# A decode layer on one core: 128 rows of w4 loaded to 16 partitions by eight two-partition loads, the rest in groups of 5, 4, 3 and 1

## The chip, the cores and the metric

The kernel runs on one core of a Trainium2 chip. The metric is device time in microseconds of one execution; the figure of a kernel is the median of several runs.

## What is computed

The reference is one decode step (sequence length 1, batch 8, D = 512): attention over the last 2048 positions of a K/V cache, then an MLP block. Cut to what matters:

```python
x = A_x                                       # [8, 1, 512]
h = x + attention(layernorm(x), k[..., -2048:, :], v[..., -2048:, :], wq, wo)
x1 = h_n + 0                                  # h_n = layernorm(h); the token-shift branch is zero for S = 1
h2 = gelu(layernorm(x1) @ w3) @ w4            # w3 [512, 1792], w4 [1792, 512]
out = h + x1 + h2
```

There are 32 query heads in 8 groups, and each group has its own K and V (head size 128). All of K, V, wq, wo, w3 and w4 that is used comes from HBM once: some 79 MB, of which w3 and w4 are 1.75 MB each. Everything is bf16, with sums in f32.

## The kernel before

One Python function writes out the instruction list of every engine by hand; `Engine.op` (L46) appends an operation with the semaphores it waits for, and `Engine.emit` (L52) writes them in that order. The engines are TensorE (`PE`), ScalarE (`AC`), VectorE (`DV`), GpSimd (`PO`) and SyncE (`SP`). SP issues every large load, in one queue, in program order.

**Ring.** `ring` (L122) has 8 slots of 2 MB. 32 loads of 2 MB, half a batch's K or V each, go round it in the order of `loads` (L292). A load into a slot waits until TensorE has used what was there (`taken`). wq and wo share another buffer. w3 and w4 go into ring slots 0 and 1 at the end: `w3_sb`, `w4_sb` (L124, L125). The order in SP's queue at the end is: the last K and V loads, four of wo, two of w3 (L669), four of w4 (L675).

**Attention.** For each of 64 steps, K is transposed on TensorE (`pe_T`, L317), evicted by ScalarE and VectorE (`evict`, L333) and multiplied by the queries (`pe_QK`, L339). The softmax is spread over the steps; GpSimd multiplies P by a mask (L384). `pe_PV` (L438) multiplies by V. `wo` follows in `pe_wo` (L543). `stream` (L593) adds filler matmuls of 512 columns at places where TensorE would wait.

**The tail.** After wo, VectorE makes the layernorm's sums (L685 to L700) and `uT`, the transposed input of w3. `pe_w3` (L705) holds 128 columns of w3 as weights and moves `uT`; w3 comes in two halves of its 512 rows, each with a semaphore, and there is one call for the first half (L715) and two for the second (L717). Its columns are taken in *chunks* of 128: as w4's load puts `r` consecutive rows of w4 on each partition, chunk `i` of a group has every `r`-th column of w3:

```python
w4_chunks += [slice(f0 + i, f0 + 128 * r, r) for i in range(r)]
dma(SP, w4_sb[:, lo:lo + r, :].rearrange("p r n -> p (r n)"),
    B_w4[f0:f0 + 128 * r, :].rearrange("(p r) n -> p (r n)", r=r), sem, w_free[1] if lo == 0 else None)
```

The groups before are r = 8, 3, 2 and 1, 14 chunks in all. The first 8 go to one PSUM bank with 64 moving columns, the other 6 to another with 32. VectorE multiplies each bank by the row scale (L738), ScalarE applies gelu (L741), and `pe_w4` (L751) holds 128 x 8 of the result as weights and moves w4, two matmuls per chunk, one for each half of the 512 outputs, on two column halves of the array. Residual and normalised input are added by `pe_fin` (L761), two filler matmuls follow (L768), then w4 group by group as it lands (L769). VectorE and ScalarE evict a half each (L774), SP stores (L778).

## Time and profile before

| | us |
|---|---|
| median of 3 runs | 193.57 (193.43 to 193.58) |
| the profiled execution | 193.76 |
| its span in the profile | 192.3 |
| TensorE busy | 159.8 (83%) |
| VectorE busy | 103.8 (54%) |
| ScalarE busy | 84.4 (44%) |
| GpSimd busy | 35.8 (19%) |
| large loads' packets, of 16 DMA engines' span | 97.0% |
| chain that ended last, DMA's share | 78% |

The profile is one execution, and its times count from the first instruction. In its rows, PE is TensorE's matmul, PEld its weight load, DVE VectorE, ACT ScalarE, POOL GpSimd, SPq the queue of SyncE; `L325` is a line of the kernel. A row of the timeline has start, duration, engine, line, operation, what is written and read, a count, and in brackets the idle time of the engine before it with what ended it. The chain of work is followed back from the last instruction, at each step to what released it. Where matmuls run one behind another, the mean duration of one (some 0.2 us) is longer than the distance of their starts, since they are pipelined; distances of starts are used for sums. Granted TensorE clock is full in the whole execution.

### The profile page before, as it was taken

Reading aid. Unit: us, or ns where it says so; the run is one execution under the profiler, and the core shown is the slowest. Engines: PE = TensorE matmul, PEld = TensorE weight load, DVE = VectorE, ACT = ScalarE, POOL = GpSimd, SP = SyncE. Lnnn points to the kernel's source line nnn. Section 1 sums busy time; section 2 is a strip of 40 time slices with the busy share of each in tenths; the row PEclk is TensorE's granted clock in tenths of the full one; section 3 lists DMA queues with packets and bytes.
Section 4 is the critical chain, followed back from the end, with each engine's and each line's share of the span. In section 5 each row is a group of like instructions: output and inputs, shape, how many; then the busy total and the mean of one; then the engine's idle time right before and its main releaser. Section 6 shows DMA issues by size and latency. Waiting matters only on the chain.

```text
span 192.3 us, 4741 instructions
## 1 busy us (share of the span) xinstructions
PE 159.8 (83%) x2108; PEld 101.8 (53%) x2108; DVE 103.8 (54%) x256; ACT 84.4 (44%) x102; POOL 35.8 (19%) x44
## 2 busy tenths in 40 slices
PE   0028999789998989998999797979998998898795
PEld 0015767567665555655656464646565653366472
DVE  7702656367457654665475546554765456552050
ACT  5002776946744544454444532454445423530040
POOL 8000000350520080008000800052004402400000
PEclk9999999999999999999999999999999999999999
DMA  6999999999999999999999999999999999999992
GB/s 220 436 423 436 433 416 433 426 428 423 436 429 433 429 433 423 426 429 431 433 423 433 429 433 429 429 433 426 424 426 429 429 433 433 423 416 430 418 381 77
DMA packets 6244, 79.47 MB, mean 413 GB/s; under 512 B 705, under 2 KB 849, under 8 KB 1361
## 3 DMA queue, kind: packets, MB, share of 16 engines
q1 hardware_dynamic: 6208, 79.18, 97.0%
q8 instruction: 16, 0.26, 0.5%
q10 hardware_dynamic: 16, 0.01, 0.0%
q14 instruction: 4, 0.02, 0.0%
HBM read 79.18 MB, written 0.01 MB: 412 GB/s over the span
## 4 chain that ended last, share of the span: by engine, by line
DMA 78%; PE 16%; DVE 2%; SPq 2%; issue 1%; ACT 0%
DMA ring<-in_A_k_cache_dram 63%; DMA ring<-in_B_w_dram 16%; PE kT_ps L325 8%; PE O_ps L445 3%; PE S_ps L345 3%; SPq L199 2%; DVE kT_sb L336 1%; PE sm L394 1%; PE sm L496 1%; DVE pT_sb L407 1%; PE S_ps L755 0%; DVE mcol L356 0%; ACT P_sb L775 0%; PE sm L360 0%; PE sm L370 0%
## 5 line engine op out<-in xcount | busy, mean ns | idle before, releaser
L334 ACT ACTIVATE kT_sb<-kT_ps 128x1024 bf16<-128x1024 bf16 x64 | 65.2, 1023 | 65.4 <-PE kT_ps L325 65.4
L325 PE MATMUL kT_ps<-ident_p,ring 128*128 128x128 bf16 x1024 | 68.3, 220 | 9.0 <-DMA ring<-in_A_k_cache_dram 7.6
L336 DVE COPY kT_sb<-kT_ps 128x1024 bf16<-128x1024 bf16 x64 | 44.3, 692 | 48.9 <-PE kT_ps L325 48.9
L325 PEld LDWEIGHTS kT_ps<-ident_p,ring 128*128 128x128 bf16 x1024 | 57.7, 98 | 22.5 <-DMA ring<-in_A_k_cache_dram 10.5
L384 POOL TENSOR_TENSOR P_sb<-P_sb,mask_b 128x512 bf16<-128x512 bf16 x30 | 31.2, 1070 | 129.2 <-ACT P_sb L374 120.1
L445 PE MATMUL O_ps<-ring,pT_sb 128*64 128x512 bf16 x208 | 31.6, 390 | 0.0
L345 PE MATMUL S_ps<-kT_sb,qwin 128*32 128x512 bf16 x256 | 26.0, 390 | 0.0
L345 PEld LDWEIGHTS S_ps<-kT_sb,qwin 128*32 128x32 bf16 x256 | 6.8, 93 | 16.3 <-issue 14.4
L394 PE MATMUL sm<-ident_s,P_sb 128*128 128x128 bf16 x120 | 11.6, 219 | 2.0 <-DVE pT_sb L407 0.7
L407 DVE COPY pT_sb<-sm 128x512 bf16<-128x512 bf16 x28 | 11.6, 415 | 1.1 <-PE sm L394 1.1
L445 PEld LDWEIGHTS O_ps<-ring,pT_sb 128*64 128x64 bf16 x208 | 7.7, 108 | 6.1 <-issue 1.6
L394 PEld LDWEIGHTS sm<-ident_s,P_sb 128*128 128x128 bf16 x120 | 7.7, 97 | 4.5 <-issue 3.6
L480 DVE SCALAR_TENSOR_TENSOR acc<-O_ps,own_f,acc 128x128 f32<-128x128 f32 x24 | 8.4, 350 | 0.8
L268 PE MATMUL S_ps<-wbig,xlnT 128*32 128x512 bf16 x32 | 3.4, 596 | 5.3 <-DMA wbig<-in_A_wq_dram 5.3
L374 ACT ACTIVATE P_sb<-S_ps,negcol 128x512 bf16<-128x512 f32 x8 | 5.5, 687 | 3.0 <-DVE negcol L373 3.0
L254 PE MATMUL sm<-ident_b,xln_b 8*128 8x8 bf16 x4 | 0.3, 174 | 7.6 <-DVE xln_b L223 7.6
L496 PEld LDWEIGHTS sm<-sum_f,acc 128*128 128x128 f32 x20 | 3.0, 188 | 6.3 <-DVE pT_sb L407 3.3
L356 DVE TENSOR_REDUCE mcol<-S_ps 128x1 f32<-128x512 f32 x8 | 5.5, 689 | 1.5 <-PE S_ps L345 1.5
L480 DVE SCALAR_TENSOR_TENSOR iota_f<-O_ps,own_f,iota_f 128x128 f32<-128x128 f32 x15 | 5.2, 348 | 1.5 <-ACT iota_f L483 1.2
L596 PE MATMUL O_ps<-kT_sb,ident_b 128*128 128x512 bf16 x21 | 5.8, 379 | 0.0
L435 DVE TENSOR_TENSOR oT_all<-sm,rL 128x16 bf16<-128x16 f32 x15 | 3.4, 229 | 4.4 <-PE sm L496 4.3
L719 ACT ACTIVATE s<-vsum,eps 128x8 f32<-128x8 f32 x1 | 0.3, 301 | 11.8 <-DVE vsum L699 11.8
(123 smaller groups left out, 109.8 us busy)
## 6 DMA issues: line engine op xcount, KB each, us to landing
ring<-in_A_k_cache_dram SPq DMA_DIRECT2D x16, 2048.0 KB, 30.7
ring<-in_A_v_cache_dram SPq DMA_DIRECT2D x16, 2048.0 KB, 26.8
wbig<-in_A_wq_dram SPq DMA_DIRECT2D x1, 4096.0 KB, 12.3
wbig<-in_A_wo_dram SPq DMA_DIRECT2D x4, 1024.0 KB, 29.9
ring<-in_B_w_dram SPq DMA_DIRECT2D x2, 896.0 KB, 34.9
ring<-in_B_w_dram SPq DMA_DIRECT2D x1, 1024.0 KB, 32.1
ring<-in_B_w_dram SPq DMA_DIRECT2D x1, 384.0 KB, 30.3
ring<-in_B_w_dram SPq DMA_DIRECT2D x1, 256.0 KB, 30.5
```

Of the source, the lines that this page charges most:

```text
L325: ins = e.matmul(kT_ps[m % 3][:, c * 128:(c + 1) * 128], ring[:, s, n * DH:(n + 1) * DH], ident_p[:, :], is_transpose=True)
L334: e_lo[i] = AC.op(lambda e: e.activation(kT_sb[:, i % NKT, 0:1024], kT_ps[2 * i % 3][:, :], ACT.Copy), e_Tlo[i], e_QK.get(i - NKT))
L336: e_hi[i] = DV.op(lambda e: e.tensor_copy(kT_sb[:, i % NKT, 1024:2048], kT_ps[(2 * i + 1) % 3][:, :]), e_Thi[i], e_QK.get(i - NKT))
L345: ins = e.matmul(S_ps[b % 2][32 * h:32 * (h + 1), :], qwin[:, b, 4 * j + h, w0:w0 + 32], kT_sb[:, i % NKT, :].rearrange("p (c h k) -> p h ...
L356: e_max[b] = DV.op(lambda e: e.tensor_reduce(mcol[:, :], S_ps[b % 2][:, :], AX.X, ALU.max), e_QK[8 * b + 7], e_mT.get(b - 1))
L374: e_exp[b] = AC.op(lambda e: e.activation(P_sb[:, :], S_ps[j][:, :], ACT.Exp, bias=negcol[:, j:j + 1], scale=1.0, accum_out=lcol[:, j:j + 1]),
L384: e_sp[b, r] = eng.op(lambda e, r=r, pb=pb, mb=mb: e.tensor_tensor(P4_sb[:, 128 * r:128 * (r + 1), :], pb, mb, ALU.mult), e_exp[b], e_PT.g ...
L394: ins = e.matmul(buf[:, x * 128:(x + 1) * 128], P4_sb[:, 32 * c:32 * (c + 1), :].rearrange("p k h -> p (k h)"), ident_s[:, :], is_transpos ...
L407: e_pT[b, r] = DV.op(lambda e: e.tensor_copy(dst, pT_ps[:, :]), e_PT[b, r], free)
L445: ins = e.matmul(bank(w)[64 * t:64 * (t + 1), :], pT_sb[:, b % NB3, c, 64 * j:64 * (j + 1)], ring[:, s, :].rearrange("p (a c d) -> p c a d ...
L480: e_part[w] = eng.op(lambda e: e.scalar_tensor_tensor(dst, src, own, dst, ALU.mult, ALU.add), e_part[w], e_PV[4 * w + 3])
L596: ins = e.matmul(O2_ps[:, :], ident_b[:, :], kT_sb[:, (NG - 1) % NKT, 0:512], start=True, stop=True)
```

## The change

Of w4's 1792 rows, the first 128 are taken out of the wide loads. Eight loads of two partitions each, 8 rows of w4 on a partition, bring them to 16 partitions (0 to 7 and 32 to 39) of a tile of 64 that GpSimd has set to zero before. The tile, and a second one for the matching columns of w3, lie in the ring slot of the last K half. SP issues the eight loads ahead of w3's. The other 1664 rows of w4 come in groups of 5, 4, 3 and 1. GpSimd copies the 128 matching columns of w3, once they have landed, to a packed tile of 8 chunks of 64 columns; columns without a row of w4 there are zero. So w3 has 13 chunks of 128 columns and 8 of 64, w4 13 chunks of 128 rows and 8 of 64 (of which 16 hold data). Order on TensorE: first group, groups two to four, small chunks in w3; in w4 the small chunks come after the first group. VectorE and ScalarE have three parts instead of two.

```diff
+        near_sb = ring[0:64, place["k", LAST, 1] % NS, 0:RW * D].rearrange("p (r n) -> p r n", r=RW)
+        near_w3 = ring[:, place["k", LAST, 1] % NS, RW * D:RW * D + KC * RW * 64].rearrange("p (k r n) -> p k r n", k=KC, r=RW)
+        e_nz = PO.op(lambda e: e.memset(near_sb, 0.0), taken["k", LAST, 1])
+        e_nw = PO.op(lambda e: e.memset(near_w3.rearrange("p k r n -> p (k r n)"), 0.0))
+        for n in range(RW):
+            p, f = 32 * (n // 4) + n % 4, 64 * (n // 4) + RW * (n % 4)
+            dst = near_sb[p:p + 5:4].rearrange("p r n -> p (r n)")
+            a = B_w4[f:f + RW, :]
+            dma(SP, dst, bass.AP(tensor=a.tensor, offset=a.offset, ap=[[4 * RW * D, 2], [1, RW * D]]), sem_near, e_nz)
...
-        w4_chunks, w4_ends, f0 = [], [], 0
-        for r, sem in zip((8, 3, 2, 1), sem_w4):
+        w4_chunks, w4_ends, f0 = [], [], 128
+        for r, sem in zip((5, 4, 3, 1), sem_w4):
...
+        e_near = [PO.op(lambda e, kc=kc: e.tensor_copy(
+            near_w3[:, kc].rearrange("p r (g n) -> p g r n", g=2)[:, :, :, 0:8],
+            w3_sb[:, kc, 0:128].rearrange("p (g n r) -> p g r n", g=2, r=RW)), (sem_w3[kc // 2], 16), e_nw)
+            for kc in range(KC)]
+        y_cols = [[lambda kc, c=c: w3_sb[:, kc, c] for c in w4_chunks[:FH]],
+                  [lambda kc, r=r: near_w3[:, kc, r, :] for r in range(RW)],
+                  [lambda kc, c=c: w3_sb[:, kc, c] for c in w4_chunks[FH:]]]
...
-        pe_w3(0, 0, FC, e_u, (sem_w3[0], 16), e_scale[LAST, 1], e_acc[NV - 2])
+        order = (0, 2, 1)
+        for n in order:
+            pe_w3(0, n, e_u, (sem_w3[0], 16), e_scale[LAST, 1], e_acc[NV - 2], e_near[1] if n == 1 else None)
         stream(1)
-        e_y = [pe_w3(1, 0, FH, (sem_w3[1], 16)), pe_w3(1, FH, FC)]
+        e_y = {n: pe_w3(1, n, (sem_w3[1], 16), e_near[3] if n == 1 else None) for n in order}
...
         for n, hi in enumerate(w4_ends):
-            e_z = pe_w4(w4_ends[n - 1] if n else 0, hi, (sem_w4[n], 16), e_gT[0 if hi <= FH else 1])
+            e_z = pe_w4(gT, w4_sb, w4_ends[n - 1] if n else 0, hi, (sem_w4[n], 16), e_gT[0 if n == 0 else 2])
+            if n == 0:
+                pe_w4(gn, near_sb, 0, RW, (sem_near, 16 * RW), e_gT[1])
```

More of the change, by code (lines that the diff above doesn't have):

```diff
@@ L193, in bass_sequential_preLN__sliding_block_cached__mixer_s_mlp__decode_kernel @@
         sem_w3 = [S(f"sem_w3{i}") for i in range(2)]
+        sem_near = S("sem_near")
         sem_w4 = [S(f"sem_w4{i}") for i in range(4)]
@@ L671, in bass_sequential_preLN__sliding_block_cached__mixer_s_mlp__decode_kernel @@
                 B_w3[256 * a:256 * (a + 1), :].rearrange("(p r) f -> p (r f)", r=2), sem, w_free[0])
-        FH = 8
-        w4_chunks, w4_ends, f0 = [], [], 0
-        for r, sem in zip((8, 3, 2, 1), sem_w4):
+        w4_chunks, w4_ends, f0 = [], [], 128
+        for r, sem in zip((5, 4, 3, 1), sem_w4):
             lo = len(w4_chunks)
@@ L681, in bass_sequential_preLN__sliding_block_cached__mixer_s_mlp__decode_kernel @@
             f0 += 128 * r
-        assert len(w4_chunks) == FC
+        FM = FC - 1
+        FH = w4_ends[0]
+        assert len(w4_chunks) == FM
         e_uz = PO.op(lambda e: e.memset(uT, 0.0), e_PT[LAST, 3])
@@ L701, in bass_sequential_preLN__sliding_block_cached__mixer_s_mlp__decode_kernel, with pe_w3 @@
                                                       ALU.mult, ALU.add))
-        y_ps, NY = [kbank[0], kbank[2]], (64, 32)
-        def pe_w3(half, lo, hi, *waits):
+        y_ps, NY, PY = [kbank[0], kbank[1], kbank[2]], (64, 32, 32), (128, 64, 128)
+        e_near = [PO.op(lambda e, kc=kc: e.tensor_copy(
[5 more added lines that the diff above has]
+                  [lambda kc, c=c: w3_sb[:, kc, c] for c in w4_chunks[FH:]]]
+        def pe_w3(half, n, *waits):
             def f(e):
-                for fc in range(lo, hi):
-                    n, f = divmod(fc, FH)
+                for f, w in enumerate(y_cols[n]):
                     for kc in (2 * half, 2 * half + 1):
-                        ins = e.matmul(y_ps[n][:, f * NY[n]:(f + 1) * NY[n]], w3_sb[:, kc, w4_chunks[fc]],
-                                       uT[:, kc, 0:NY[n]], start=(kc == 0 and f == 0), stop=(kc == KC - 1),
-                                       skip_group_check=True)
+                        ins = e.matmul(y_ps[n][0:PY[n], f * NY[n]:(f + 1) * NY[n]], w(kc), uT[:, kc, 0:NY[n]],
+                                       start=(kc == 0 and f == 0), stop=(kc == KC - 1), skip_group_check=True)
                 return ins
             return PE.op(f, *waits)
-        pe_w3(0, 0, FC, e_u, (sem_w3[0], 16), e_scale[LAST, 1], e_acc[NV - 2])
+        order = (0, 2, 1)
+        for n in order:
+            pe_w3(0, n, e_u, (sem_w3[0], 16), e_scale[LAST, 1], e_acc[NV - 2], e_near[1] if n == 1 else None)
         stream(1)
-        e_y = [pe_w3(1, 0, FH, (sem_w3[1], 16)), pe_w3(1, FH, FC)]
+        e_y = {n: pe_w3(1, n, (sem_w3[1], 16), e_near[3] if n == 1 else None) for n in order}
         e = AC.op(lambda e: e.activation(s2[:, :], vsum[:, :], ACT.Sqrt, bias=eps2[:, :], scale=(1.0 + EPS) / D), e_vs)
@@ L728, in bass_sequential_preLN__sliding_block_cached__mixer_s_mlp__decode_kernel, with bcf @@
         e_fin = DV.op(lambda e: e.tensor_tensor(f_lo[:, :], fin[:, :], f_hi[:, :], ALU.subtract), e)
-        def bcf(t, n):
-            a = t[:, :]
+        def bcf(t, n, p):
+            a = t[0:p, :]
             return bass.AP(tensor=a.tensor, offset=a.offset, ap=[a.ap[0], [0, n], [1, B]])
-        e_gT = []
-        for n in range(2):
-            fn = (FH, FC - FH)[n]
-            cs = slice(n * FH * B, (n * FH + fn) * B)
-            e = DV.op(lambda e, n=n, cs=cs, fn=fn: e.tensor_tensor(v3(g_x[:, cs]),
-                y_ps[n][:, 0:fn * NY[n]].rearrange("p (f w) -> p f w", w=NY[n])[:, :, 0:B], bcf(r2, fn),
-                                                                   ALU.mult), e_y[n], e_r2)
-            e_gT.append(AC.op(lambda e, cs=cs: e.activation(gT[:, cs], g_x[:, cs], ACT.Gelu_apprx_tanh), e))
+        gn_x = P4_sb[0:64, 96:128, :].rearrange("p k h -> p (k h)").bitcast(dt.float32)
+        gn = P4_sb[0:64, 64:80, :].rearrange("p k h -> p (k h)")
+        halves = [slice(0, FH * B), slice(FH * B, FM * B)]
+        g_parts = [(g_x[:, halves[0]], gT[:, halves[0]]), (gn_x, gn), (g_x[:, halves[1]], gT[:, halves[1]])]
+        e_gT = {}
+        for n in order:
+            gx, g = g_parts[n]
+            fn = len(y_cols[n])
+            y = y_ps[n][0:PY[n], 0:fn * NY[n]].rearrange("p (f w) -> p f w", w=NY[n])[:, :, 0:B]
+            e = DV.op(lambda e, gx=gx, y=y, fn=fn, n=n: e.tensor_tensor(v3(gx), y, bcf(r2, fn, PY[n]), ALU.mult), e_y[n], e_r2,
+                      e_PT[LAST, 3])
+            e_gT[n] = AC.op(lambda e, gx=gx, g=g: e.activation(g, gx, ACT.Gelu_apprx_tanh), e)
         z_ps = S_ps[1]
@@ L749, in rows, with pe_w4 @@
             return ins
-        def pe_w4(lo, hi, *waits):
+        def pe_w4(g, w, lo, hi, *waits):
             def f(e):
@@ L754, in f @@
                     for a in range(2):
-                        ins = e.matmul(z_ps[64 * a:64 * a + B, 0:256], gT[:, fc * B:(fc + 1) * B],
-                                       w4_sb[:, fc, 256 * a:256 * (a + 1)].rearrange("p (j r) -> p r j", r=2),
-                                       start=False, stop=(fc == FC - 1), tile_position=(0, 64 * a), skip_group_check=True)
+                        ins = e.matmul(z_ps[64 * a:64 * a + B, 0:256], g[:, fc * B:(fc + 1) * B],
+                                       w[:, fc, 256 * a:256 * (a + 1)].rearrange("p (j r) -> p r j", r=2),
+                                       start=False, stop=(w is w4_sb and fc == FM - 1), tile_position=(0, 64 * a), skip_group_check=True)
                 return ins
```

## The prediction

> **What bounds the kernel now.** I read the 40 slices first, then the chain of work that ended last, then the timeline of its last 8 us, then the DMA queues, and last the packet records and semaphore increments behind them.

> ```profile
> DMA  6999999999999999999999999999999999999992
> ...
> q8 instruction: 16, 0.26, 0.5%
> ```

> The 16 DMA engines are busy from the second slice to the last but one. The chain of waits ends so:

> ```profile
> 159.31 30.47 DMA ring<-in_B_w_dram
> 189.78 0.04 issue
> 189.82 0.61 PE S_ps L755 x6
> 190.43 0.02 issue
> 190.45 0.45 ACT P_sb L775
> ```

> The third piece of w4 (256 rows) lands at 189.78, the fourth at 190.09; only six matmuls, the eviction and the store follow. Around it the timeline shows:

> ```profile
> 185.57 1.45 PE L710 MATMUL kT_ps<-P_sb,ring 128*128 128x64 bf16 x28 [0.36 <-DMA ring<-in_B_w_dram]
> ...
> 187.28 0.61 PE L596 MATMUL O_ps<-kT_sb,ident_b 128*128 128x512 bf16 x2
> 187.99 0.77 PEld L755 LDWEIGHTS S_ps<-ring,gT 128*8 128x8 bf16 x16 [0.59 <-DMA ring<-in_B_w_dram]
> ...
> 190.13 0.09 PEld L755 LDWEIGHTS S_ps<-ring,gT 128*8 128x8 bf16 x2 [0.22 <-DMA ring<-in_B_w_dram]
> ```

> TensorE starts the second half of w3 when it lands (185.57), has the filler matmuls done by about 187.72 and waits for w4's first piece until 187.99. So it has some 0.27 us of slack there and short waits after each piece.

> The 16 engines do not end together. The last w4 load's increments come at 186.7, 186.8, 186.8, 186.9, 186.9, 187.1, 187.4, 188.3 and then eight between 189.6 and 190.1. The packet records say why. An engine takes 4.86 us for its eight 16 KB packets of a 2 MB load. Each of the 16 packets on q8 (16 KB of TensorE's instructions) makes the engine it falls on 1.41 to 1.42 us late, and they fall on eight engines in turn, two each. Those eight end late. The other eight have none; on two of them smaller instruction fetches cost 0.55 us (one) and 1.67 us (two).

> **What the change removes.** 128 KB leaves the wide w4 loads, 8 KB per engine. From packet starts, 8, 3, 2 and 1 KB packets take 306, 118, 80 and 42.5 ns, so 8 x (306+118+80+42.5) = 4.37 us of w4 per engine. With pieces of 5, 4, 3, 1 rows (5 and 4 KB interpolated: 193 and 155) it is 8 x 508 = 4.07. All engines but two end **0.30 us earlier**: landings at about 187.25 (5 rows), 188.50, 189.44 and 189.79.

> **What it adds to DMA.** Each small load has two 8 KB rows. The 8-row x load used eight engines (its semaphore gets one step at issue and eight later), so two rows should use two: 8 x (306+6) = **2.50 us** for each, ahead of w3 in the queue, 2.20 net of the cut. [...]

> Which two decides. By the packets that follow x's, x's eight engines are four undisturbed ones, the two with small fetches, and two with two TensorE fetches (neighbours in the fetch order). I take an undisturbed pair: its second w3 half lands at 182.3 to 182.8 now and at most 185.3 after, still before 185.53, and its w4 ends by 189.3. Then w3's landing stays and w4's last is 189.79.

> **SP and POOL queues.** The memset of near_sb waits for the last K transposes (155.1). By the row of qwin it takes 4096/3840 x 3.29 = 3.5 us, to 158.6; near_w3's 1.8 us more, to 160.4, ahead of the P multiply at 162.27.

> ```profile
> 1.59 3.29 POOL L213 MEMSET qwin<- 128x3840 bf16 x1
> ```

> SP holds the eight small loads, w3 and w4 behind that wait: eight issues at 0.4 (x's and w4's rows: 0.37 to 0.6) end at about 162. w3 was issued at 148.8 to 154.5, but its packets start only when wo is done, about 178, so 15 us of cover remain. w4's third issue already takes 11.0 us for want of queue room; 16 more descriptors on two engines that are ahead delay it by a few us at most, under the same cover.

> **TensorE.** w3, per half: now 16 matmuls at 60 ns (weights strided by 8 columns) and 12 at 26 (strides 3, 2, 1), 1.30 us. After: 10 at stride 5, unknown between 27 and 60, I take 45; 8 at stride 4, same bounds, I take 30, near stride 3; 8 at 26; 16 packed with 64 columns, between 25 (128 packed columns, wo) and 58 (twice the 29 ns of the 32-column loads at L534), I take 30. Sum 0.45+0.24+0.21+0.48 = 1.38; bounds 1.09 to 2.2. So +0.1 (-0.2 to +0.9), all of it on the path from 185.57.

> w4: 14 pairs become 21. A pair starts 113 ns after the one before, 64-row pairs too, since their moving side is as long. Filler ends at 187.82, first pair about 187.95; the first piece has been there since 187.25, so TensorE no longer waits for DMA. Twenty steps: 187.95 + 2.27 = 190.22. The small pairs use 64 rows, w3's use 64 columns: changes of shape. Nearest row:

> ```profile
> 148.25 0.55 PE O_ps L445 x4
> 148.80 0.33 PE S_ps L345 x4
> ```

> Four 512-column matmuls in two pairs need 2 x 0.213 = 0.43 and take 0.55: 0.12 per change at most, nothing at least; three changes, I take 0.1 in all. [...] Last pair: **190.3 against 190.13 now, +0.2**; the cut of 0.30 in DMA buys nothing, because TensorE is last by then.

> **POOL's copies.** Four copies of 128 elements a partition; no such row. Bounds: the 128-element memset, 0.19, and the 512-element multiply, 1.07; I take 0.3, near a quarter of the latter. Two follow w3's second landing: 185.53 + 0.6 = 186.2; TensorE wants them at about 186.5 (after 26 matmuls). Over 0.45 us each they come late. The first two face w3's first half, which has 0.15 us of slack before 185.57. [...]

> DVE and ACT get one more small operation each (0.21 and 0.25 us, rows L738 and L741): the last gelu ends near 187.7, before the small pairs at 188.5. TensorE gains 84 records; a seventeenth fetch, one per 256 records, would come in the last 30 and hit nothing.

> **Sum.** Removed 0 (hidden), added 0.2 net at the end: from the profiled execution's 193.76 us (span 192.3) to 193.96; from the median 193.57 to **193.8**. Bounds of the unknown terms: 193.4 to 194.4.

> **Rivals.**
> - *The two engines are late ones* (slower). Their w3 increments now come from 185.23 on; +2.50 makes 187.73, 2.20 after today's 185.53, and the whole path moves: 193.57 + 2.2 + 0.2 = **196.0**. It decides from the point where an engine has under 2.2 us in hand. For it: two of x's eight engines are such. Against: six are not. [...]
> - *One of the two has the small fetches.* 183.95 + 2.50 = 186.45, 0.92 late: **194.7**.
> - *POOL's copies end last*: at 1.0 us each, 187.5 instead of 186.5: **194.8**.
> - *TensorE hides its 0.2* (the packed weights save more than the pairs cost): DMA's end counts, -0.3 at best: **193.3**.
> [...]

> **How the numbers follow.** 0.2% is 0.39 us, about what a measurement of this kernel can tell from no change. Engines in neighbouring pairs: two of x's four pairs are undisturbed, one has small fetches (of which only one engine matters much), one is late. I give the undisturbed case 0.55, small fetches 0.15, late 0.25, POOL 0.05. Within the undisturbed case: 0.04 under 193.18, 0.40 within 0.2%, 0.11 above 193.96. So faster 0.04, same 0.40, slower 0.11+0.15+0.25+0.05 = 0.56. The likeliest case alone reaches 193.4 to 194.4; to leave out under 2 in 10 the range must take in most of the late case: 193.4 to 196.1.

> **What would show it.** Right: the second w3 half still starts at 185.6, L755's pairs run without a DMA wait from 187.95 and end at 190.3. Late engines: w3 starts at 187.7. Late POOL: TensorE idles before the last sixteen w3 matmuls with POOL as releaser. Wrong altogether: w4's pairs wait for DMA again, or the start of w3 moves earlier.

## The result and the profile after

| | before | after |
|---|---|---|
| median, us (6 runs each on one chip) | 193.47 | 194.66 (194.40 to 194.84) |
| ratio, 95% interval | | 1.0061 (1.0048 to 1.0074) |
| the profiled execution, us | 193.76 | 194.84 |
| its span, us | 192.3 | 193.2 |
| last w4 landing, us of the span | 190.09 | 189.72 |
| last pair of w4 matmuls starts | 190.13 | 191.01 |

The changed kernel is 1.19 us slower. One execution of the last experiment's kernel (199.73 us, mean granted clock 0.966) was in a slower state of the chip and is left out of that kernel's ratio and means. The wide loads do end earlier, by 0.37, and TensorE ends 0.88 later. The 40 slices and the instruction queue of the page after:

```profile
DMA  6999999999999999999999999999999999999980
...
q8 instruction: 16, 0.26, 0.5%
```

The last slice of the DMA line was 2 tenths and is 0. Part of that is the longer span, by which the slice starts 0.9 later, but the landings in the table say the same: DMA is done before TensorE. The chain that ended last now runs through TensorE (start, duration, engine, what is written, line; helper lines moved down a little, w3's matmuls are L728, the filler L597, `pe_fin` L770, w4's L778):

```profile
185.69 1.66 PE kT_ps L728 x42
187.35 0.32 PE S_ps L770 x8
187.67 0.16 issue
187.83 0.38 PE O_ps L597
188.21 1.09 PE S_ps L778 x15
189.30 0.15 issue
189.45 1.86 PE S_ps L778 x27
191.31 0.02 issue
191.33 0.45 ACT P_sb L800
```

No DMA stands between w3's second half and the eviction, and in the middle of w4 there is a piece of "issue": TensorE waited for nothing that the profile shows. The timeline of the same stretch:

```profile
185.69 0.79 POOL L716 COPY ring<-ring 128x128 bf16<-128x128 bf16 x2 [1.38 <-DMA ring<-in_B_w_dram]
...
188.14 0.73 PE L778 MATMUL S_ps<-ring,gT 128*8 128x256 bf16 x10
188.80 1.48 PE L778 MATMUL S_ps<-ring,P_sb 64*8 64x256 bf16 x16
189.45 0.54 PEld L778 LDWEIGHTS S_ps<-ring,P_sb 64*8 64x8 bf16 x10 [0.45 <-issue]
190.21 1.07 PE L778 MATMUL S_ps<-ring,gT 128*8 128x256 bf16 x16
```

Sixteen matmuls on 128 rows take 1.07 us; the sixteen small ones take 1.48. The fifth and the sixth are a pair, and a pair's two matmuls start within 0.01 us of each other; here 0.42 us lie between them (189.03 to 189.45). I call such a gap a **hole**. There is a second one in `wo`, from 181.80 to 182.09. By count of TensorE's records they lie at about 4031 and 4285, 254 apart (five matmul records are missing from the trace), and they end 2.4 and 2.3 us after a 16 KB packet starts on q8, the page's instruction queue (at 179.70 and 187.19). I read these packets as TensorE's instructions: from the first of the sixteen to the last TensorE goes from 328 records to 4233, 260 from one packet to the next on the mean. Before, the kernel has 4258 counted records, so a boundary at 4285 would have come after its end.

### The profile page after: what moved, and what is told of

Same layout as the page of the kernel before. It is cut to its first block, busy times and chain, and to the rows that moved or that the text cites. A ratio compares the mean times of both kernels' runs of the same rounds, so it can differ in the third digit from the quotient of the medians.

```text
span 193.2 us, 4837 instructions
## 1 busy us (share of the span) xinstructions
PE 162.1 (84%) x2145; PEld 104.6 (54%) x2150; DVE 104.2 (54%) x257; ACT 84.7 (44%) x103; POOL 42.6 (22%) x50
## 4 chain that ended last, share of the span: by engine, by line
DMA 54%; PE 36%; DVE 4%; ACT 3%; SPq 1%; issue 1%
DMA ring<-in_A_k_cache_dram 31%; DMA wbig<-in_A_wo_dram 17%; PE kT_ps L326 17%; DMA wbig<-in_A_wq_dram 6%; PE S_ps L346 5%; PE O_ps L446 4%; DVE kT_sb L337 2%; PE S_ps L269 2%; PE kT_ps L728 2%; ACT kT_sb L335 2%; PE S_ps L778 2%; SPq L200 1%; PE sm L395 1%; ACT L375 1%; PE sm L371 1%
## 5 line engine op out<-in xcount | busy, mean ns | idle before, releaser
L326 PE MATMUL kT_ps<-ident_p,ring 128*128 128x128 bf16 x1024 | 69.6, 222 | 7.3 <-DMA ring<-in_A_k_cache_dram 5.9
L326 PEld LDWEIGHTS kT_ps<-ident_p,ring 128*128 128x128 bf16 x1024 | 59.1, 99 | 20.4 <-issue 8.1
L738 ACT ACTIVATE s<-vsum,eps 128x8 f32<-128x8 f32 x1 | 0.3, 302 | 12.3 <-DVE vsum L710 12.3
L497 PE MATMUL sm<-sum_f,acc 128*128 128x16 f32 x20 | 4.0, 273 | 1.7 <-DVE pT_sb L408 1.4
```

The source lines that it names most:

```text
L326: ins = e.matmul(kT_ps[m % 3][:, c * 128:(c + 1) * 128], ring[:, s, n * DH:(n + 1) * DH], ident_p[:, :], is_transpose=True)
L497: e_oT[w] = PE.op(lambda e: e.matmul(oT_ps[:, hh], acc[w % 3][:, :], sum_f[:, :], start=True, stop=True), e_acc[w], e_sum, small[0])
```

## The experiments

Three theories were on trial. **W** (work): the loss is the sum of the added matmuls and shape changes. **F** (fetch): a block of 256 TensorE instructions arrives late, at a fixed count of records, and TensorE stands still until it is there. **D** (DMA engines): one or two DMA engines end late.

### Seven of eight small chunks left out

```diff
-                pe_w4(gn, near_sb, 0, RW, (sem_near, 16 * RW), e_gT[1])
+                pe_w4(gn, near_sb, 0, 1, (sem_near, 16 * RW), e_gT[1])
```

The rows of w4 behind those chunks are not added.

> Leaves out seven of the eight small chunks in the w4 product (14 of 16 small matmuls), so the output lacks their part; all loads, copies and the w3 product stay. Theory W (TensorE's own work in w4 makes the loss): seven pairs of 113 ns and little else go, TensorE is no longer last and the kernel ends with DMA, 0.3 to 0.6 us under the kernel before or level with it, some 193.2 to 193.5 us. Theory F (TensorE waits for its instructions at one place in every 256 records, about 2.3 us after the fetch): the same place of the program is now in the last two groups, a hole of up to 0.4 us stays there: 193.5 to 193.8. Theory D (the two engines' extra loads delay the end): no change, 194.6.

Measured: 193.52 us, ratio 1.0009 (0.9997 to 1.002); ten of the eleven runs lie between 193.32 and 193.84, one at 194.64. The last landing is 189.74, as in the changed kernel. So the late end does not come from DMA (against D). A hole remains, from 189.13 to 189.45, after a q8 packet at 187.19; it stands at a later matmul of the source, since fewer records come before it, but ends at the same time. The time alone fits W and F; the hole is what F expected and W did not.

### No filler ahead of w4

```diff
         PE.op(pe_fin, e_fin, e_exp[LAST], e_scale[LAST, 1])
-        stream(2)
```

> The two filler matmuls ahead of w4 are taken out; nothing else. Theory W: TensorE is the bound from w3's second half on, so the 0.45 us of filler come off: 194.2. Theory F: the fetch that the hole in w4 waits for starts in w3's second half, before the filler, so TensorE only reaches the hole earlier and waits longer: hole 0.6 to 0.9 us instead of 0.42, time 194.5 to 194.7. Theory D: no change, 194.6.

Measured: 194.68 us, ratio 1.0066 (1.0052 to 1.0079), no gain in the median. But the runs fall into two groups: 193.63 and 193.81, and five from 194.66 to 195.10. The profiled one is the fastest, and its timeline is that of a kernel without a hole:

```profile
187.34 0.74 PE L778 MATMUL S_ps<-ring,gT 128*8 128x256 bf16 x10
...
188.01 1.07 PE L778 MATMUL S_ps<-ring,P_sb 64*8 64x256 bf16 x16
...
189.01 1.07 PE L778 MATMUL S_ps<-ring,gT 128*8 128x256 bf16 x16
```

w4 starts 0.80 earlier (0.16 of it because w3's second half landed earlier in this execution, so 0.64 by the filler), and the small matmuls take 1.07. The sixteenth q8 packet came at 185.05 here instead of 187.19. W fails: 0.64 us of TensorE's path were taken away and five of seven runs are no faster. F explains both groups: where the block comes at 189.45, an earlier start only makes TensorE wait longer for it. (For the five longer runs there is no trace; that they had the hole is inferred from the time.)

### Small tiles of 128 rows and columns

```diff
-        near_sb = ring[0:64, place["k", LAST, 1] % NS, 0:RW * D].rearrange("p (r n) -> p r n", r=RW)
+        near_sb = ring[:, place["k", LAST, 1] % NS, 0:RW * D].rearrange("p (r n) -> p r n", r=RW)
...
-        y_ps, NY, PY = [kbank[0], kbank[1], kbank[2]], (64, 32, 32), (128, 64, 128)
+        y_ps, NY, PY = [kbank[0], kbank[1], kbank[2]], (64, 32, 32), (128, 128, 128)
```

The tile of w3's columns and the small gelu tile grow in the same way; the added rows and columns are zero.

> The small tiles are made full: 128 rows (112 of them zero) and 128 columns, so that no matmul has 64 rows or 64 columns; the number of matmuls, the loads and the copies stay. Theory W with shape changes: the three changes of shape measured 0.08, 0.10 and 0.09 us go, and 16 weight loads of w3 take 25 ns instead of 32: 0.3 to 0.4 us less, 194.3. Theory F: the hole stays, only what lies before the fetch's start and behind the hole counts: 0.1 to 0.25 less, 194.4 to 194.55. If shape changes cost nothing here: 194.6.

Measured: 194.11 us, ratio 1.0038 (1.0023 to 1.0052), again two groups (193.84 to 194.15, and 194.67 and 194.74). The profiled run (194.15) had its sixteenth q8 packet at 185.19 and no hole:

```profile
188.10 0.73 PE L778 MATMUL S_ps<-ring,gT 128*8 128x256 bf16 x10
188.67 1.07 PE L778 MATMUL S_ps<-ring,P_sb 128*8 128x256 bf16 x16
189.57 1.07 PE L778 MATMUL S_ps<-ring,gT 128*8 128x256 bf16 x16
```

From the small group to the next it is 0.90 here (189.57 less 188.67) and 1.00 in the run without filler (189.01 less 188.01), and from the first group to the small one 0.57 against 0.67: the change to 64 rows and back costs some 0.10 us each way. w3's second half, from its start to `pe_fin`, takes 1.38 us here (185.86 to 187.24), as before, against 1.59 in the changed kernel.

### Twenty records more at the start

Ten matmuls of 8 columns, each with its weight load, ahead of the first real matmul, where TensorE waits for x:

```diff
+        def pe_idle(e):
+            for _ in range(10):
+                ins = e.matmul(O2_ps[:, 0:8], ident_b[:, :], ident_b[:, 0:8], start=True, stop=True)
+            return ins
+        PE.op(pe_idle, e_idb)
         e = PE.op(pe_xT, e_xln, e_idb)
```

> Ten tiny matmuls (128x8, 20 records) are put at the very start, while TensorE waits for wq; the tail's work is the same. Theory W and D: no change, 194.6. Theory F: every hole moves 20 records earlier in the program; the one in w4 moves from the small group to the first group (from about 189.0 to 188.3) and the one in wo by as much; the time moves with it, 0.0 to 0.5 us up.

Measured: 195.29 us, ratio 1.0091 (1.0077 to 1.0105), 0.63 over the changed kernel where 0.5 at most was expected. Both holes moved twenty records ahead and grew, to 0.62 in `wo` and 0.77 in w4:

```profile
182.08 0.64 PE L554 MATMUL S_ps<-oR,wbig 128*128 128x32 bf16 x19 [0.44 <-issue]
...
188.30 0.51 PE L783 MATMUL S_ps<-ring,gT 128*8 128x256 bf16 x6
189.30 0.39 PE L783 MATMUL S_ps<-ring,gT 128*8 128x256 bf16 x4 [0.49 <-issue]
189.62 1.07 PE L783 MATMUL S_ps<-ring,P_sb 64*8 64x256 bf16 x16
```

The hole sits now in the first group of w4 (after its sixth matmul), 2.19 us after a q8 packet at 187.11. Nothing in the tail was edited. By count the two holes are at 4034 and 4290, where they were in the changed kernel (4031 and 4285, with five records missing), though other matmuls stand there now; no record is missing here, and the distance is 256. W has no room for this; it is the strongest evidence for F. It also holds both ways over all fourteen profiles, in which TensorE passes these two places 25 times (missing records added to the count). Seven times it gets there 1.0 to 2.1 us after the start of the packet that belongs to the place (the fifteenth or the sixteenth) and stands until 2.2 to 2.4 us after it; the other eighteen times it gets there 2.4 us or more after, and does not stand.

### The same on the kernel before: forty matmuls

> The kernel before with 40 tiny matmuls (80 TensorE records) added at its start, where TensorE waits for data; nothing else changes, and none of the change is in it. Theory F (a TensorE instruction block of 256 records that is fetched too late): the boundary that lies some 29 records past the end of the kernel before moves to some 51 records ahead of the end, into w4's second pair. If that block's fetch starts at 187.1 as in the changed kernel, the block is there at about 189.4, twelve to thirteen pairs are left, the last pair starts near 190.85 instead of 190.13, and the time is about 194.2 (ratio up to 1.004); if the fetch starts at 185.1, as in two of the earlier runs, there is no hole and no loss: 193.5. So 193.5 to 194.3, with a gap of issue in w4 wherever it is over 193.8. Theory W (the 1.19 us is the sum of the change's own matmuls and shape changes): the tail of the kernel before is untouched, 193.5 in every run, no gap.

Measured: 193.55 us, ratio 1.0002 (0.9993 to 1.001). No hole: the sixteenth q8 packet came at 182.74 and the seventeenth at 189.29. The expectation allowed this, and it tells nothing for or against F beyond one thing: eighty records more cost nothing where both blocks come in time.

### 130 records more on the changed kernel

> The changed kernel with 65 tiny matmuls (130 records) at its start. Theory F: the boundary that lay in the small chunks of w4 moves to the start of w3's second half, where TensorE waits for w3's landing anyway, and the next one lies some 70 records past the end; w4 then runs without a hole of issue. Last pair near 190.55 instead of 191.01, time about 194.1 to 194.25 (ratio 1.0035), if the block for w3's second half is there by 185.7; if it comes later, w3's second half starts that much later and the time shows it one for one. Theory W: nothing of the tail is changed, 194.66 as the changed kernel.

Measured: 194.66 us, ratio 1.0058 (1.0046 to 1.007): the hole is gone as F said, and the time is not. The timeline:

```profile
188.74 1.07 PE L783 MATMUL S_ps<-ring,P_sb 64*8 64x256 bf16 x16
189.74 0.62 PE L783 MATMUL S_ps<-ring,gT 128*8 128x256 bf16 x8
190.74 0.62 PE L783 MATMUL S_ps<-ring,gT 128*8 128x256 bf16 x8 [0.38 <-DMA ring<-in_B_w_dram]
```

The small group is whole, and now the third piece of w4 is late. Its increments end 189.33, 189.34 and then a single one at 190.69; the fourth piece's end 189.65, 189.67, 190.96. One DMA engine is 1.3 us behind fifteen. The queue shows the cause:

```profile
q8 instruction: 17, 0.28, 0.5%
```

The seventeenth fetch came at 187.96. A fetch makes its DMA engine 1.41 us late (before, w4's last piece ends on six engines between 186.67 and 187.10 and on eight between 189.61 and 190.09, by the medians 2.9 apart for two fetches each), sixteen fall on eight engines twice each, and this one makes an engine late a third time (that it is a third time on one engine is inferred: the packet records name none). So D, wrong for the changed kernel, is right for this one. The other boundary makes a hole here too, at the counted record 4032, from 177.35 to 177.99 in `wo`, where it costs nothing.

### The same with one small chunk

> The changed kernel with seven of the eight small chunks of w4 left out (the rows of w4 behind them are not added), and 65 tiny matmuls at its start. It was 193.52 without them, with a hole of issue of 0.31 us just before its last groups. Theory F: that hole goes, TensorE catches up with w4's pieces, and the end is set by the last piece's landing at 189.72 instead of 190.09: 193.1 to 193.25, ratio 0.998 or 0.9985. It shows what the shorter wide loads would be worth if TensorE hid its part. Theory W: 193.52 again, ratio 1.000.

Measured: 194.88 us, ratio 1.0065 (1.0052 to 1.0078), a miss by 1.7 us. The same rule: the seventeenth fetch came at 188.40, the third piece's last increment is alone at 190.64 (the one ahead of it 189.57), and the last eight matmuls wait for it from 189.79 to 190.68. TensorE had little to do here and lost as much. The hole at record 4032 lasts 1.33 us (177.54 to 178.87, in `wo`).

### Four rows on 32 partitions, loaded after w3

```diff
-        for n in range(RW):
-            p, f = 32 * (n // 4) + n % 4, 64 * (n // 4) + RW * (n % 4)
-            dst = near_sb[p:p + 5:4].rearrange("p r n -> p (r n)")
...
+        for n in range(16):
+            p, f = 32 * (n // 8) + n % 8, 64 * (n // 8) + NR * (n % 8)
+            dst = near_sb[p:p + 9:8].rearrange("p r n -> p (r n)")
```

`NR` is 4, and the loop stands behind w3's two loads.

> The changed kernel with 4 rows of w4 on each of 32 partitions instead of 8 on 16: sixteen two-partition loads instead of eight (4 KB rows, the same bytes), issued after w3's loads instead of ahead of them, and four small chunks instead of eight, so four pairs of matmuls less in w4 and sixteen small matmuls less in w3. Work: w3's half 0.25 shorter than in the changed kernel, w4 0.45 shorter; last pair by work alone near 189.85, last landing 189.72 if the same two engines take the small loads. Theory F: 48 records fewer put the block boundary within the last seven records, where a block that is there at 189.5 comes in time: no hole, 193.2 to 193.5. Theory W (the whole 1.19 us is work, 0.17 us for each added pair): four pairs less give 0.68 less, 194.0.

Measured: 195.27 us, ratio 1.0102 (1.0073 to 1.013), a miss by 1.8 us. The one trace is of the longest execution (197.11 us, span 194.6); the other five took 194.93 to 195.30 with spans of 193.4 to 193.8, so it shows more than they lost. In it TensorE's work was less, but w4's first piece was late:

```profile
188.99 1.23 PE L779 MATMUL S_ps<-ring,gT 128*8 128x256 bf16 x10 [1.11 <-DMA ring<-in_B_w_dram]
```

Its increments end 187.12, 187.18 and then 188.95. Again one engine, 1.7 to 1.8 us late in all four pieces (the last 191.41 against 189.71). The increments of the small loads show which: they step in two chains of sixteen, one from 182.64 to 185.47, the other from 183.43 to 187.67, and w4 lies behind them in the queue. So one of the two engines was no longer ahead: it came to the small loads later and took 0.28 us a row where the other took 0.19. Why its rows were slow is not shown. That is the prediction's rival of a late engine, in another kernel. The granted clock fell too, from 1.00 to 0.50 at 188.85, in the wait of 1.11 us (0.50 in both microseconds from 189 to 191), and w4's pairs went at 0.23 us instead of 0.113. What the other five executions waited for is not shown.

### No filler at all

`stream` adds nothing (21 matmuls, 42 records) in three kernels: the changed one, the changed one with one small chunk (the other rows of w4 not added), and the kernel before.

> The changed kernel without any of its 21 filler matmuls (42 TensorE records; they compute nothing that is used). Theory F (late instruction block): the boundary that lay 57 records ahead of the end lies some 15 ahead, where a block that comes at 189.4 is in time, and no 17th fetch comes early enough to delay a DMA engine; the tail runs as in the one undisturbed profile without the last filler: w4 from 187.35, small chunks from 188.0, last groups from 189.0, last pair near 189.85. So 193.6 in nearly every run, instead of 193.6 or 194.7 by turns, ratio 0.9995 to 1.0015. Theory W (the 1.19 us is the work of the change alone): the last filler in front of w4 is 0.7 us of the path, so 194.0, without gaps. If the fillers kept TensorE's clock up, the granted clock falls under 1.0 and the time is longer than both.

> The same without fillers, and with seven of the eight small chunks of w4 left out (the rows of w4 behind them are not added). No block boundary is left near the end and TensorE has less to do than w4's landings leave time for. Theory F, and the step of the prediction that the shorter wide loads end 0.30 us earlier: last pair after the last landing at 189.72, against 190.09 before, so 193.1 to 193.25, ratio 0.998 to 0.9988. If a landing of w4 is later than 189.8 (theory D, a DMA engine with one fetch more than the others), 193.5 or more, and the increments show which.

> The kernel before without its 21 filler matmuls: the control for the two others. The filler in front of w4 lies in a wait for w4's first piece, and the end is set by DMA: all theories expect 193.5, ratio 0.999 to 1.001, if the fillers do nothing for TensorE's clock; if they do, the granted clock falls and the w4 pairs after the last landing take longer, at most some 0.3 us.

Measured: 196.84, 194.83 and 194.16 us; ratios 1.0156 (1.0137 to 1.0176), 1.007 (1.0055 to 1.0084) and 1.003 (1.002 to 1.004). All three missed the likelier expectation, for the reason that two of them named; the kernel before lost 0.65, twice the 0.3 that its expectation allowed for the clock. The clock in the 40 slices of the first:

```profile
PEclk9999999999999999999999999999999999985555
```

From 174.5 to the end it is 0.50. Its w4 took 1.79 us for the eight small pairs (189.72 to 191.51) instead of 1.00. No hole appears in any of the three, and their last landings are 189.65, 189.73 and 190.20, so the shorter wide loads show up here too; but the clock hides what they would give.

### Full rows, no filler ahead of w4, 70 records more

The three edits together: the tiles of 128 rows, no `stream(2)` ahead of w4, 35 of the tiny matmuls at the start.

> Three edits of the changed kernel together: 128 rows and columns in the small tiles (no change of shape), no filler in front of w4 (the 19 earlier ones stay, so the granted clock should stay at 1.0), and 35 tiny matmuls (70 TensorE records) at the start. Theory F: the block boundary of the tail moves into w3's second half, with its fetch asked for before w3's first, and the next fetch comes after 188.9; if the first is there by 186.7 and the second hits no engine with w4 still to bring, w4 starts near 187.3, its 21 pairs take 20 x 0.113 = 2.26, and the last one waits for the last landing at 189.6 to 189.8: 193.1 to 193.4, ratio 0.998 to 0.9995. If the first comes up to 1.0 us late, there is a hole in w3's second half and the time is up to 194.3; if the second comes at 188.0 to 188.6, the third or fourth piece of w4 lands near 190.7 and the time is near 194.3. Theory W, with the filler's 0.7 and the shape changes' 0.2 off the 1.19: 193.75, without gaps.

Measured: 193.54 us, ratio 1.0001 (0.9992 to 1.0011), where F expected 193.1 to 193.4. In the trace all came as F said: fetches at 182.80 and 189.31, no hole, last landing 189.75 with no engine apart from the others, and TensorE waiting for DMA again:

```profile
187.29 0.74 PE L783 MATMUL S_ps<-ring,gT 128*8 128x256 bf16 x10
...
189.36 0.21 PEld L783 LDWEIGHTS S_ps<-ring,gT 128*8 128x8 bf16 x6 [0.28 <-DMA ring<-in_B_w_dram]
189.80 0.09 PEld L783 LDWEIGHTS S_ps<-ring,gT 128*8 128x8 bf16 x2 [0.23 <-DMA ring<-in_B_w_dram]
```

The last pair starts at 189.80, 0.33 ahead of the kernel before. Yet the time is the same. The gain went outside the span. The mean span is 191.97 over ten runs against 192.19 for the kernel before (61 runs over the four sets of experiments), 0.22 less; but the time outside the span, device time less span, is 1.58 against 1.33, 0.25 more.

## Why the prediction was right in kind, in part by luck, and 0.86 us short

"Slower" (0.56) and the wide range held, but not for the reasons given: 0.45 of the 0.56 and all of the range above 194.4 were there for late engines and a late POOL, and neither came. That 194.66 lies in the range is luck. The forecast itself, 193.8, and the undisturbed case's own range (193.4 to 194.4) did not hold. Step by step, against the profiled executions:

**DMA end, right.** Predicted 187.25, 188.50, 189.44 and 189.79; measured 187.17, 188.42, 189.40 and 189.72. From w3's second landing to w4's last it takes 4.56, 4.37 and 4.39 in three profiles of the old loads and 3.98 to 4.13 in eight of the changed kernel and its variants (all but the three with a late engine). The 0.30 is real.

**The two engines, right in effect, wrong for one of them.** The semaphore of the small loads steps in two interleaved chains of eight (178.45 to 180.69 and 179.07 to 181.32), 0.32 us from step to step: two engines, as forecast. That all eight loads fall on the same two, on which the 2.50 rests, was my estimate; no row of before shows it, and the two chains do. But they are not an undisturbed pair. In w4's last piece six engines ended between 186.7 and 187.1 before, and one each at 187.4 and 188.3; now five end between 186.5 and 186.9, and three between 188.5 and 189.3, ahead of the eight late ones (189.3 to 189.7). So one of the two is an undisturbed engine, and the other is the one at 187.4, with a single small fetch. Followed by the starts of its packets, it takes its small loads from 178.53 to 181.01 and ends w3 at 185.64 and w4 at 189.72, the last of all sixteen, where I had 185.3 and 189.3 at most. Its w3 landed at 183.05 before, and by the prediction's own sum 183.05 + 2.50 = 185.55 is level with the 185.53 at which all of w3 was there: that w3's landing stayed (185.64; it wanders from 185.4 to 185.8 between executions) was luck on this engine.

**POOL and SP, right in effect, wrong in size.** The memsets stand behind the P multiply in POOL's order and ran at 165.13 and 168.62, not at 155; SP issued the small loads from 168.70 on at 0.56 to 0.72 each (I took 0.4) and was done with w4 at 176.6. w4's third issue took 0.43 here, with 731 packets of the queue issued and not yet done at its start, where it took 11.0 before with 1297. wo's loads landed until 181.2, so the cover held, with less to spare than the 15 us I counted. The copies took 0.42 where 0.3 was taken, the last two 0.79 together, done at 186.49; TensorE asked for them at 186.67.

**w3, small miss.** From its start to `pe_fin` the half took 1.59 against 1.38 before, +0.20 where +0.1 was forecast (16 matmuls at 60 ns and 12 at 26 are 1.27, not the 1.30 that I put for before). The strides were near (5: 40 ns, 45 taken; 4: 33, 30 taken) and, as the run with full columns shows, cost nothing over before; the 64 columns cost it all: 32 ns a load (30 taken; 25 with full columns), and the first two start 0.11 and 0.05 us after the matmul ahead of them, 0.10 in all over the usual distance.

**Shape changes, mis-sized.** I took 0.1 for all; w4's two cost 0.19 (the run with full rows has none of it), w3's 0.10. The most that the row of before allows, 0.12 for each of three changes, is 0.36, and the sum of 0.29 lies nearer to it than to 0.1.

**w4's start, late by 0.19.** 188.14 instead of 187.95: w3's second half starts 0.11 later than before and takes 0.1 longer than forecast. The later `pe_fin` passes straight on through the filler. Its two matmuls lay in a wait before; now their cover is gone, and without them w4 started 0.64 earlier. I had them on the path, but did not say that 0.6 us of the path were filler.

**The step that failed: "a seventeenth fetch, one per 256 records, would come in the last 30 and hit nothing."** The trace of before shows 260 records from one packet to the next on the mean (295 to 4190 in fifteen steps); the 256 shows in a later run, as the distance of two holes with no record missing. I asked which DMA engine a further fetch would hit, and not when TensorE would need the block. With 84 records more, the block boundary that had lain past the end (at about 4285, where the kernel before has 4258 records) falls into w4's small chunks. No seventeenth fetch was needed for that; the sixteenth, at 187.19, was too late. The hole of 0.42 is the largest part of the miss in the profiled execution; for the other five there is no trace. With it the sum closes: 0.19 (start) + 0.09 (shapes in w4 over what was taken) + 0.42 (hole) = 0.70, and the last pair is 191.01 against the forecast 190.3.

**Outside the span, not considered.** I carried the 1.46 us between span and time over unchanged. It is 1.64 in the profiled execution after, and in the mean of all runs 1.55 (six runs) against 1.33. All twelve other kernels agree with their kind: 1.35 for the two made from the kernel before, 1.48 to 1.69 for those made from the changed one. 0.70 and 0.18 make the 0.88 between 193.96 and 194.84. What of the change causes it is not settled: it does not go with the eight additional matmul chunks (1.52 with one of them) nor with added instructions alone (1.35 with 40 matmuls more on the kernel before). That one was not tried further.

**The rivals.** None of them was what happened. Two were priced close to the measured 194.66, the small fetches (194.7) and the late POOL (194.8), but their signs are missing: w3's second half starts at 185.69 and not after 186.4, and POOL's copies are done before TensorE asks for them. The late engine appeared in the kernel with four rows alone. "TensorE hides its 0.2" was built at the end (193.54): there the 0.3 us is visible in the trace and does not reach the time.

**Still open.** What decides whether the sixteenth fetch starts at about 185.1 or at 187.0 to 187.2, with all else equal. From the moment when TensorE passes record 4034, 256 ahead of the place where the block is needed, it takes 3.0 to 3.7 us in nine profiles and 5.0 to 5.3 in five, the changed kernel's among them.

## What to carry to other kernels

## What the runs showed of the hardware that was not expected

**Instruction blocks.** Seven holes, of 0.29 to 1.33 us, in five kernels (the changed one, with one chunk, with 20 records more, and the two with 130): all at a count of 4031 to 4034 or 4285 to 4290 records, whatever instruction stands there, and all over 2.2 to 2.4 us after a q8 packet starts. A fetch that starts at 187.96 or 188.40 leaves one DMA engine behind all others at w4's third piece, by 1.35 and 1.07 us; one at 189.2 to 189.4 (four kernels) does no harm. The two holes of one trace lie 254 records apart in the changed kernel (five missing) and 256 with 20 records more (none missing), near the 260 from one packet to the next; eighteen of the 25 passings have no hole, seven have one.

**The clock.** In the three kernels without filler the granted clock fell to 0.50 at 174.49, 173.60 and 176.64 and stayed there for 13.7 us or more, though in the first of them TensorE worked 4.11 of the 7 us from 176 to 183. No single wait explains it: the first fall comes where a wait of 1.20 us only begins, the second 1.3 us ahead of one, the third behind one, and the changed kernel waited 1.73 us (116.32 to 118.05) at a clock of 1.00. But within each trace the changes of the clock lie whole multiples of 3.41 us apart (without filler and with one chunk, 173.60 to 190.67 is five of them and to 194.08 six; with four rows, 188.85 to 192.27 is one). What sets the clock at these steps, and how little work makes it fall, is not settled. In the kernel with four rows TensorE was busy 2.11 us of the 3.41 ahead of the fall, and the kernel before had 2.07 from 115.16 to 118.58 without one.
